# A new order table for an attention and gated-MLP kernel: 419 of 1883 operations at other places on their engines

## The chip, the cores and the metric

The kernel runs on one core of a Trainium2 chip. The metric is the device time of one execution in microseconds, taken as the median of several runs; lower is better. The engines are called TensorE (PE; its weight load is PEld), VectorE (DVE), ScalarE (ACT), GpSimd (POOL) and SyncE (SP, which issues the DMAs).

## The reference

Causal attention over 4 batches, 12 heads, 448 positions and 64 dimensions a head, and behind it a gated MLP (d_model 768, d_ff 1024) on the attention's output, all in float32:

```python
scores = scale * np.matmul(q, k.transpose(0, 1, 3, 2))
scores = np.where(mask, -1000000000.0, scores)
attn = np.exp(scores - np.max(scores, axis=-1, keepdims=True))
attn = attn / (np.sum(attn, axis=-1, keepdims=True) + 1e-09)
x = (attn @ v)   # heads side by side: (4, 448, 768)
h = x @ w_in                                   # 768 -> 1024
h = 0.5 * h * (1.0 + np.tanh(c * (h + 0.044715 * h ** 3)))
u, v = (h[..., :d_ff // 2], h[..., d_ff // 2:])
v_n = (v - mu) / np.sqrt(var + 1e-06) * g_ln   # over the 512 columns
v_s = np.einsum('ts,bsd->btd', w_sg, v_n) + b_sg[None, :, None]
return x + (u * v_s) @ w_out
```

## The kernel before

**Attention.** The 48 heads are worked on as 24 pairs, six to a batch (`pair(p)`). For a pair, TensorE makes the scores (L431), VectorE adds the mask and takes the maximum (L446), ScalarE takes the exponential with its sum (L454). VectorE turns the sums into reciprocals (L464 to L466), which go through DRAM (L473, L476) to come back as rows `rb`. The probabilities are transposed by TensorE for the first eight pairs (L498, evicted at L503 and L505) and by VectorE's stream transpose with four DMAs for the others (L486, L490). TensorE multiplies with v (L524), VectorE scales with `rb` into `xt` (L551). `keep_x` then splits `xt` into a high part (L557 on GpSimd in batch 0, L559 on ScalarE behind it) and low parts on GpSimd (L560, L562).

**Gated MLP.** `mlp(b)` runs after the six pairs of a batch in the code, and beside the pairs of the next batch in the table. All its products are made of high and low parts, three matmuls for one, through `group` (L579), in pieces of three matmuls. There are four v chunks of rows (three of 128, the last of 64), four u chunks, four groups of the spatial mix (weights `vn` of all four v chunks, against `wsg`) and six output groups. The gelu is four steps: square on ScalarE (L587), VectorE (L588), tanh on ScalarE (L590), VectorE (L592). The last v chunk is joined from two halves first (L613 on ScalarE, L615 on VectorE). The layer norm of a v chunk is a chain over three engines: statistics (L619, L620) and L621 on VectorE, a power on GpSimd (L623), L625 on VectorE, the normalising on ScalarE (L628), the high part on ScalarE (L632; L637 for the last chunk), and the low part on GpSimd (L633) for the first three chunks, but on VectorE (L638) for the last. The spatial mix needs all of these; its results go through L671 (VectorE), L675 (GpSimd), L677 (ScalarE) and L678 (GpSimd). The residual is summed on GpSimd (L691), added to the output group on VectorE (L704), and stored by DMA (L708).

**Weights.** They are loaded and split in the first 105 us: L364, L366, L368, L370, L373, L374 for the input and output weights, L352 and L353 for the spatial weights.

**What sets the order.** Each `od.add` above records an operation with its engine and what it reads and writes. Nothing is emitted until the end, where `run` goes through the numbers of the table ORDER (L67 and the lines below it) and emits operation after operation. So each engine's queue is the table restricted to its operations, each engine works strictly in that order, and buffers and PSUM banks are handed out in that order too.

Of the kernel before, what the change touches and what calls it, by code (L numbers as in the profile page):

```python
# [66 lines left out]
    0, 1, 3, 4, 84, 85, 125, 2, 89, 87, 90, 96, 86, 126, 127, 12, 18, 166, 24, 344, 350, 116, 157, 207, 88, 95, 98,  # L67
    97, 91, 93, 92, 99, 94, 101, 130, 128, 14, 129, 103, 132, 100, 13, 15, 16, 17, 134, 104, 102, 105, 106, 133, 131,
    30, 248, 356, 107, 136, 19, 110, 108, 109, 138, 140, 111, 135, 141, 167, 171, 169, 20, 168, 5, 6, 26, 21, 22, 23,
    173, 172, 170, 137, 142, 143, 145, 139, 144, 146, 7, 8, 9, 10, 114, 115, 112, 11, 149, 25, 27, 28, 29, 208, 178,  # L70
    177, 113, 180, 179, 174, 181, 31, 175, 176, 182, 184, 185, 186, 150, 210, 211, 218, 183, 32, 33, 34, 35, 117, 118,
    119, 120, 121, 122, 123, 124, 209, 216, 151, 152, 153, 190, 212, 214, 215, 217, 187, 220, 154, 222, 147, 36, 37,
    223, 213, 219, 155, 156, 224, 226, 225, 221, 227, 191, 358, 362, 364, 346, 38, 42, 44, 39, 40, 41, 584, 249, 253,
    251, 158, 159, 160, 161, 289, 148, 162, 163, 164, 585, 165, 192, 196, 194, 233, 193, 195, 234, 231, 235, 232, 236,
    228, 254, 260, 197, 252, 259, 237, 238, 250, 257, 290, 198, 255, 258, 256, 292, 291, 296, 293, 294, 262, 188, 48,
    49, 623, 50, 51, 261, 298, 52, 264, 265, 263, 268, 267, 266, 300, 43, 302, 53, 297, 304, 299, 305, 306, 239, 199,
    200, 240, 229, 54, 189, 241, 242, 243, 201, 202, 203, 204, 206, 205, 664, 308, 269, 295, 301, 440, 274, 278, 279,
    272, 441, 230, 244, 45, 46, 47, 245, 246, 247, 309, 276, 307, 303, 310, 332, 335, 338, 368, 270, 280, 321, 313,
    273, 314, 315, 316, 319, 320, 275, 317, 318, 624, 628, 626, 629, 625, 632, 630, 665, 333, 334, 336, 277, 635, 339,
    637, 337, 340, 442, 311, 631, 638, 640, 669, 627, 670, 634, 642, 351, 636, 633, 281, 282, 283, 284, 271, 285, 322,  # L80
    323, 324, 325, 374, 375, 376, 56, 370, 667, 668, 312, 326, 286, 287, 327, 328, 666, 673, 671, 672, 674, 352, 55,
    57, 639, 345, 363, 365, 347, 60, 66, 353, 62, 643, 641, 644, 354, 355, 458, 443, 676, 678, 675, 61, 647, 330, 380,
    386, 705, 744, 648, 677, 680, 459, 444, 341, 445, 446, 447, 679, 684, 63, 377, 388, 681, 682, 683, 655, 696, 645,
    685, 686, 448, 449, 58, 68, 382, 67, 357, 359, 69, 348, 349, 651, 649, 653, 460, 654, 461, 462, 463, 464, 690,
    691, 650, 646, 783, 392, 687, 398, 59, 70, 72, 706, 707, 342, 360, 361, 343, 366, 367, 404, 465, 708, 652, 466,
    712, 713, 709, 467, 710, 714, 711, 720, 722, 716, 718, 724, 717, 450, 468, 451, 469, 470, 452, 688, 689, 369, 476,
    477, 478, 479, 480, 692, 693, 694, 719, 695, 715, 723, 387, 721, 725, 481, 482, 371, 729, 745, 746, 749, 747, 753,
    748, 755, 453, 471, 751, 64, 65, 78, 754, 762, 757, 760, 764, 454, 455, 752, 483, 381, 759, 71, 288, 389, 656,
    697, 657, 658, 659, 660, 735, 410, 698, 699, 700, 329, 701, 750, 730, 731, 733, 734, 472, 378, 379, 372, 373, 416,
    422, 732, 456, 457, 484, 485, 756, 758, 383, 74, 406, 73, 79, 761, 75, 394, 76, 77, 384, 385, 784, 785, 792, 790,  # L90
    786, 494, 495, 496, 497, 498, 499, 726, 727, 486, 787, 405, 473, 80, 487, 793, 788, 763, 393, 399, 474, 475, 500,
    791, 798, 794, 395, 400, 488, 81, 489, 789, 501, 502, 82, 83, 390, 391, 490, 768, 396, 397, 491, 796, 423, 801,
    492, 493, 503, 769, 504, 505, 512, 522, 513, 514, 523, 424, 418, 425, 506, 507, 407, 428, 430, 412, 401, 532, 542,
    524, 533, 534, 535, 536, 525, 543, 526, 515, 516, 517, 544, 545, 546, 661, 795, 429, 797, 411, 508, 431, 413, 417,
    419, 402, 420, 403, 663, 802, 527, 518, 528, 800, 509, 510, 822, 1044, 434, 519, 520, 529, 511, 521, 765, 432,
    552, 537, 560, 561, 562, 538, 530, 539, 540, 531, 799, 553, 554, 555, 331, 547, 548, 556, 563, 770, 772, 736, 737,
    738, 739, 773, 771, 807, 774, 775, 776, 777, 778, 426, 408, 409, 433, 414, 557, 415, 662, 541, 549, 564, 803, 808,
    435, 421, 565, 427, 550, 551, 558, 559, 566, 823, 824, 831, 827, 825, 832, 838, 826, 436, 437, 829, 766, 728, 568,
    569, 570, 740, 830, 833, 835, 840, 842, 813, 852, 571, 576, 572, 577, 837, 839, 841, 438, 439, 567, 573, 828, 834,
    836, 578, 579, 580, 581, 1045, 1047, 1046, 586, 587, 574, 575, 582, 702, 583, 1053, 1051, 804, 811, 812, 810, 809,  # L100
    846, 847, 1048, 1055, 1057, 703, 1052, 1061, 1049, 1050, 1059, 1056, 1063, 591, 599, 600, 601, 592, 602, 767, 704,
    779, 597, 603, 588, 589, 593, 594, 1054, 595, 1062, 843, 1058, 604, 605, 606, 607, 1083, 1122, 1084, 805, 1161,
    598, 590, 608, 1085, 1123, 1088, 1086, 1087, 1060, 741, 743, 611, 780, 1064, 782, 1094, 848, 849, 850, 806, 851,
    1092, 1089, 1095, 1097, 1093, 1099, 1101, 1096, 844, 845, 814, 815, 816, 817, 853, 854, 1074, 1068, 1069, 1070,
    1073, 855, 856, 1113, 1072, 1125, 1126, 1133, 1135, 1071, 612, 617, 618, 619, 620, 613, 614, 615, 742, 818, 1090,
    1091, 1098, 781, 1127, 1128, 857, 610, 819, 1103, 621, 1124, 1129, 1162, 1100, 1102, 1104, 1131, 1105, 1163, 1200,
    609, 1134, 1136, 1065, 1066, 1132, 616, 1239, 1107, 1108, 1111, 861, 862, 863, 864, 820, 865, 858, 859, 1138, 866,
    867, 1170, 1166, 1171, 1179, 868, 1130, 869, 1177, 1181, 1140, 1137, 879, 870, 871, 872, 1168, 1167, 873, 1173,
    874, 1169, 1164, 880, 881, 882, 883, 884, 885, 1178, 886, 887, 1142, 1141, 1175, 1139, 897, 898, 899, 900, 901,
    902, 915, 916, 903, 1165, 1172, 1176, 1180, 1174, 888, 904, 905, 1110, 1109, 1112, 1146, 1067, 1106, 596, 1075,  # L110
    1114, 1115, 1076, 1077, 1078, 1147, 1150, 1148, 1149, 1151, 1116, 1117, 860, 821, 1079, 1118, 889, 875, 890, 876,
    906, 907, 891, 908, 909, 877, 878, 1201, 1202, 1240, 1207, 1143, 1208, 1205, 917, 918, 919, 920, 1206, 892, 893,
    1242, 894, 895, 896, 1209, 1210, 1185, 1203, 1144, 1152, 1191, 1186, 1190, 1189, 1217, 1212, 1214, 1204, 921,
    1216, 1215, 1219, 922, 923, 1182, 1244, 933, 934, 935, 936, 937, 943, 938, 944, 945, 946, 953, 947, 948, 963, 964,
    1005, 1080, 910, 911, 912, 913, 914, 1082, 924, 1245, 925, 1243, 1251, 1220, 1253, 1250, 1211, 926, 1213, 954,
    955, 956, 957, 965, 939, 940, 949, 927, 950, 928, 929, 1006, 1081, 1188, 1187, 1218, 951, 1224, 1225, 1221, 966,
    958, 1153, 1154, 1155, 1192, 1018, 1461, 1500, 1145, 1183, 1184, 1193, 1194, 1156, 1195, 1230, 1269, 1226, 1229,
    1228, 1227, 941, 1252, 1119, 1120, 1121, 1019, 967, 968, 930, 931, 942, 932, 959, 969, 952, 973, 974, 975, 976,
    977, 1157, 1158, 960, 961, 970, 971, 962, 978, 972, 979, 981, 982, 983, 984, 985, 989, 990, 1196, 1241, 1462,
    1463, 1248, 1249, 1255, 1257, 1246, 1247, 1222, 1539, 1259, 1256, 1254, 1258, 986, 980, 987, 991, 992, 993, 994,  # L120
    997, 998, 999, 1000, 1001, 988, 1007, 1012, 1020, 1021, 1025, 1008, 1013, 1002, 995, 996, 1003, 1022, 1014, 1004,
    1015, 1023, 1263, 1264, 1268, 1266, 1265, 1578, 1267, 1468, 1469, 1476, 1478, 1470, 1464, 1465, 1472, 1474, 622,
    1260, 1471, 1477, 1480, 1466, 1467, 1473, 1475, 1479, 1481, 1026, 1027, 1016, 1261, 1009, 1028, 1024, 1029, 1030,
# [644 lines left out]
```

## Time and profile before

| | us |
|---|---|
| median of 3 runs | 337.73 (336.57 to 338.04) |
| profiled execution, its own time | 336.46 |
| span of the profiled execution | 334.7 |
| TensorE busy in it | 323.1 |
| VectorE, ScalarE, GpSimd busy | 253.4, 207.9, 173.5 |

The profile is of one execution; its own time is 1.8 us above its span. Times in rows count from the start of the span. A row of a timeline gives start, duration, engine, line, operation and shape, and in brackets how long the engine was idle before and what ended that. TensorE is the engine with the most work and is idle for 11.6 us of the span.

### The profile page before, as it was taken

Reading aid. Unit: us, or ns where it says so; the run is one execution under the profiler, and the core shown is the slowest. Engines: PE = TensorE matmul, PEld = TensorE weight load, DVE = VectorE, ACT = ScalarE, POOL = GpSimd, SP = SyncE. Lnnn points to the kernel's source line nnn. Section 1 sums busy time; section 2 is a strip of 40 time slices with the busy share of each in tenths; the row PEclk is TensorE's granted clock in tenths of the full one; section 3 lists DMA queues with packets and bytes.
Section 4 is the critical chain, followed back from the end, with each engine's and each line's share of the span. In section 5 each row is a group of like instructions: output and inputs, shape, how many; then the busy total and the mean of one; then the engine's idle time right before and its main releaser. Section 6 shows DMA issues by size and latency. Waiting matters only on the chain.

```text
span 334.7 us, 7589 instructions
## 1 busy us (share of the span) xinstructions
PE 323.1 (97%) x2591; PEld 265.6 (79%) x2591; DVE 253.4 (76%) x762; ACT 207.9 (62%) x674; POOL 173.5 (52%) x225
## 2 busy tenths in 40 slices
PE   5799999999999999999989999999999999999995
PEld 3467768768988978878878987878988888889994
DVE  4998989999999897879698778778899422547503
ACT  3999999898857566565865537583686301465400
POOL 4366795686879852103474627051527805062690
PEclk9999999999999999999999999999999999999998
DMA  6988989587757856947757397658345451010104
GB/s 217 358 277 264 282 210 292 165 254 173 207 156 183 254 159 162 285 130 187 178 175 191 46 299 181 176 168 209 98 128 153 101 152 58 0 55 2 55 0 166
DMA packets 34326, 56.95 MB, mean 170 GB/s; under 512 B 9456, under 2 KB 18416, under 8 KB 34288
## 3 DMA queue, kind: packets, MB, share of 16 engines
q1 hardware_dynamic: 34288, 56.47, 59.4%
q8 instruction: 20, 0.33, 0.4%
q14 instruction: 18, 0.15, 0.1%
HBM read 33.39 MB, written 6.29 MB: 119 GB/s over the span
## 4 chain that ended last, share of the span: by engine, by line
PE 83%; DVE 7%; ACT 4%; DMA 3%; issue 1%; POOL 1%; SPq 0%; DVEq 0%; ACTq 0%; POOLq 0%
PE m L579 61%; PE o L524 10%; PE s L431 10%; ACT P L454 3%; DMA rb<-rd 2%; PE tx L498 1%; DMA qk<-in_qk_dram 1%; PE ty L498 1%; DVE s L446 1%; DVE vn L638 1%; DVE g L368 1%; DVE P L486 1%; DVE vn L370 1%; DVE xt L551 1%; POOL win L374 0%
## 5 line engine op out<-in xcount | busy, mean ns | idle before, releaser
L454 ACT ACTIVATE P<-s,ngm 64x64 f32<-64x64 f32 (+3 forms) x240 | 101.1, 436 | 32.5 <-DVE ngm L446 27.8
L446 DVE CUSTOM_DVE_ANT_0 s<-s,mask 64x64 f32<-64x64 f32 (+3 forms) x192 | 76.9, 438 | 9.7 <-PE s L431 7.8
L579 PE MATMUL m<-win,x 128*128 128x512 f32 (+1 forms) x264 | 65.7, 397 | 0.0
L579 PE MATMUL m<-x,win 128*128 128x448 f32 x288 | 61.7, 367 | 0.0
L579 PE MATMUL m<-g,wout 128*128 128x448 f32 x288 | 61.2, 367 | 0.0
L579 PEld LDWEIGHTS m<-x,win 128*128 128x128 f32 x288 | 54.0, 188 | 5.5
L579 PEld LDWEIGHTS m<-g,wout 128*128 128x128 f32 x288 | 53.9, 188 | 4.9
L579 PEld LDWEIGHTS m<-win,x 128*128 128x128 f32 (+1 forms) x264 | 47.2, 183 | 10.9
L431 PE MATMUL s<-qk 64*64 64x64 f32 (+5 forms) x768 | 45.3, 370 | 5.3 <-DMA qk<-in_qk_dram 4.5
L454 ACT ACTIVATION_READ_ACCUMULATOR P<-s,ngm 128x1 f32 (+1 forms) x240 | 50.3, 210 | 0.0
L431 PEld LDWEIGHTS s<-qk 64*64 64x64 f32 x768 | 29.9, 139 | 21.4 <-issue 9.5
L524 PE MATMUL o<-B,vraw 128*64 128x64 f32 (+4 forms) x672 | 45.3, 291 | 0.0
L524 PEld LDWEIGHTS o<-B,vraw 128*64 128x64 f32 x672 | 33.4, 137 | 13.1 <-issue 5.1
L486 DVE STREAM_TRANSPOSE P<-P 128x1024 f32<-128x1024 f32 x32 | 38.5, 1226 | 2.9 <-DMA B<-P 2.9
L579 PE MATMUL m<-wsg,vn 128*128 128x448 f32 x176 | 38.7, 368 | 1.2 <-DVE vn L638 1.2
L579 PEld LDWEIGHTS m<-wsg,vn 128*128 128x128 f32 x176 | 32.6, 188 | 4.6 <-DVE vn L638 1.6
L623 POOL TENSOR_TENSOR mv<-mv,mhalf 128x1 f32<-128x1 f32 (+1 forms) x16 | 10.3, 645 | 47.0 <-DVE mv L621 32.9
L560 POOL TENSOR_TENSOR x<-xt,x 128x448 fp32r<-128x448 f32 x24 | 27.4, 1149 | 12.9 <-ACT x L559 12.5
L691 POOL TENSOR_TENSOR res<-x 128x448 f32<-128x448 f32 x24 | 27.2, 1146 | 10.8 <-DMA out_dram<-res 10.8
L704 DVE TENSOR_TENSOR res<-m,res 128x448 f32<-128x448 f32 (+1 forms) x25 | 14.6, 600 | 22.3 <-PE m L579 13.6
L590 ACT ACTIVATE tmp<-tmp 128x448 f32<-128x448 f32 (+2 forms) x32 | 19.1, 601 | 15.3 <-DVE tmp L588 15.2
L588 DVE SCALAR_TENSOR_TENSOR tmp<-tmp,m 128x448 f32<-128x448 f32 (+1 forms) x28 | 17.7, 640 | 14.0 <-ACT tmp L587 13.8
(76 smaller groups left out, 395.6 us busy)
## 6 DMA issues: line engine op xcount, KB each, us to landing
B<-P SPq DMA_DIRECT2D x64, 256.0 KB
qk<-in_qk_dram SPq DMA_DIRECT2D x24, 448.0 KB
vn<-in_w_in_dram SPq DMA_DIRECT2D x12, 512.0 KB
vraw<-in_vP_dram SPq DMA_DIRECT2D x24, 256.0 KB
rb<-rd SPq DMA_DIRECT2D x24, 224.0 KB
out_dram<-res SPq DMA_DIRECT2D x9, 448.0 KB
g<-in_w_out_dram SPq DMA_DIRECT2D x16, 192.0 KB
out_dram<-res SPq DMA_DIRECT2D x5, 224.0 KB
```

Of the source, the lines that this page charges most:

```text
L431: nc.tensor.matmul(out=s[z][bk].t[64 * h:64 * h + 64, col:col + n], lhsT=qk_.t[r, 0, q0:q0 + 64], rhs=qk_.t[r, 1, k0:k0 + n], start=True, ...
L446: nc.vector.tensor_tensor_reduce(out=o, in0=i, in1=mk, scale=-0.125, scalar=3e38, op0=ALU.add, op1=ALU.min, accum_out=ngm[ib[z]][c][0:m])
L454: act(n, lambda c=c, m=m, k0=k0, n=n, bk=bk, col=col, off=off, kc=kc, i=i, z=z: nc.scalar.activation(out=P[i][0:m, off:off + n], in_=s[z][ ...
L486: dve(PW, lambda z=z: nc.vector.transpose(A[ia][:, :, :, z, :].rearrange("p g t k -> p t g k"), P[ib[z]]), Pk[z] + [kp], Ak, 1.105)
L524: nc.tensor.matmul(out=dst(o.t[r]), lhsT=vr.t[:, c, r], rhs=src(z), start=first and n == 0, stop=last and n == len(lst) - 1)
L560: pool_tt(S, lambda: nc.gpsimd.tensor_tensor(out=y.t[:, S + 64:], in0=x.t, in1=f(y.t)[:, 0:S], op=ALU.subtract), [x, y], [(y, 1)])
L579: nc.tensor.matmul(out=ps.t[0:l().shape[1], 0:n], lhsT=l(), rhs=rr(), start=(k == 0), stop=(k == len(mms) - 1))
L588: dve(n, lambda: nc.vector.scalar_tensor_tensor(out=z(), in0=z(), scalar=1.0 / GC, in1=h(), op0=ALU.add, op1=ALU.mult), [ps], [t])
L590: act(n, lambda: nc.scalar.activation(out=z(), in_=z(), func=AF.Tanh, scale=GS * GC), [], [t], True)
L623: od.add("pool", 0.46, lambda mv=mv, m=m: nc.gpsimd.tensor_tensor(out=mv.t[0:m, 1:2], in0=mv.t[0:m, 1:2], in1=mhalf[0:m], op=ALU.pow), ["s ...
L691: pool_tt(S, lambda rr=rr, x=x, k=k: nc.gpsimd.tensor_tensor(out=rr.t[:, k, :], in0=f(x.t)[:, 0:S], in1=f(x.t)[:, S + 64:], op=ALU.add), [ ...
L704: dve(hi - lo, lambda rr=rr, ps=ps, z=z, lo=lo, hi=hi: nc.vector.tensor_tensor(out=rr.t[:, z, lo:hi], in0=ps.t[:, lo:hi], in1=rr.t[:, z, l ...
```

## The change

Only the table ORDER is replaced. The program records the same 1883 operations; 419 of them stand at another place in the queue of their engine: 65 on TensorE, 147 on VectorE, 121 on ScalarE, 36 on GpSimd and 50 on SyncE. The new table comes from a search that replayed orders, half of the replays with measured and half with modelled durations and landings. Two lines of the diff, whose numbers say nothing by themselves:

```diff
 ORDER = (
-    0, 1, 3, 4, 84, 85, 125, 2, 89, 87, 90, 96, 86, 126, 127, 12, 18, 166, 24, 344, 350, 116, 157, 207, 88, 95, 98,
+    0, 4, 2, 1, 3, 84, 85, 125, 89, 86, 87, 12, 166, 18, 24, 116, 157, 344, 207, 350, 126, 90, 96, 88, 95, 91, 93, 92,
```

The first place is VectorE at the last v chunk of batch 1 (near 164 to 176 us before), where `mv` is the layer norm's mean and variance, `tmp` a gelu's working tile, `P` the probabilities and `vn` the normalised chunk. Before:

```order
474 L620 BN_AGGR mv<-st 64x2
475 L588 SCALAR_TENSOR_TENSOR tmp<-tmp,m 128x448
476 L621 TENSOR_SCALAR mv<-mv 64x1
477 L588 SCALAR_TENSOR_TENSOR tmp<-tmp,m 128x448
478 L625 TENSOR_SCALAR mv<-mv 64x1
479 L486 STREAM_TRANSPOSE P_92<-P_90 128x8x4x32 x2
480 L464 TENSOR_REDUCE tot<-sm_118 128x8
481 L465 RECIPROCAL rs<-tot 128x8
482 L466 STREAM_TRANSPOSE rT_123<-rs 128x64
483 L592 SCALAR_TENSOR_TENSOR g<-tmp,m 128x448
484 L638 TENSOR_TENSOR vn_2454<-tmp,vn_2454 64x512
```

After:

```order
479 L620 BN_AGGR mv<-st 64x2
480 L621 TENSOR_SCALAR mv<-mv 64x1
481 L588 SCALAR_TENSOR_TENSOR tmp<-tmp,m 128x448 x2
482 L486 STREAM_TRANSPOSE P_92<-P_90 128x8x4x32 x2
483 L625 TENSOR_SCALAR mv<-mv 64x1
484 L592 SCALAR_TENSOR_TENSOR g<-tmp,m 128x448
485 L464 TENSOR_REDUCE tot<-sm_118 128x8
486 L465 RECIPROCAL rs<-tot 128x8
487 L466 STREAM_TRANSPOSE rT_123<-rs 128x64
488 L638 TENSOR_TENSOR vn_2429<-tmp,vn_2429 64x512
```

L621 moved ahead of the first L588, and L625 behind the two L486. On GpSimd at the same place, before:

```order
126 L562 TENSOR_TENSOR x<-xt,x 128x64
127 L623 TENSOR_TENSOR mv<-mv,mhalf 64x1
128 L691 TENSOR_TENSOR res<-x 128x448
129 L560 TENSOR_TENSOR x<-xt,x 128x448
130 L691 TENSOR_TENSOR res<-x 128x448
131 L560 TENSOR_TENSOR x<-xt,x 128x448
132 L562 TENSOR_TENSOR x<-xt,x 128x64
133 L691 TENSOR_TENSOR res<-x 128x448
```

After:

```order
125 L562 TENSOR_TENSOR x<-xt,x 128x64
126 L691 TENSOR_TENSOR res<-x 128x448
127 L623 TENSOR_TENSOR mv<-mv,mhalf 64x1
128 L560 TENSOR_TENSOR x<-xt,x 128x448
129 L691 TENSOR_TENSOR res<-x 128x448
130 L560 TENSOR_TENSOR x<-xt,x 128x448
131 L691 TENSOR_TENSOR res<-x 128x448
132 L562 TENSOR_TENSOR x<-xt,x 128x64
```

One L691 moved ahead of L623, and the last L691 ahead of L562. On ScalarE there, the L628 and L632 of the third v chunk moved ahead of an L559. The third place is VectorE at the last v chunk of batch 2 (near 240 to 247 us before). Before:

```order
625 L619 BN_STATS st<-tmp 64x6
626 L620 BN_AGGR mv<-st 64x2
627 L621 TENSOR_SCALAR mv<-mv 64x1
628 L588 SCALAR_TENSOR_TENSOR tmp<-tmp,m 128x448
629 L446 ISA s,ngm_99<-s,mask 128x320
630 L446 ISA ngm_99 128x1
631 L625 TENSOR_SCALAR mv<-mv 64x1
632 L638 TENSOR_TENSOR vn_3225<-tmp,vn_3225 64x512
633 L588 SCALAR_TENSOR_TENSOR tmp<-tmp,m 128x448
634 L592 SCALAR_TENSOR_TENSOR g<-tmp,m 128x448
```

After:

```order
631 L619 BN_STATS st<-tmp 64x6
632 L588 SCALAR_TENSOR_TENSOR tmp<-tmp,m 128x448
633 L620 BN_AGGR mv<-st 64x2
634 L621 TENSOR_SCALAR mv<-mv 64x1
635 L446 ISA s,ngm_99<-s,mask 128x320
636 L446 ISA ngm_99 128x1
637 L625 TENSOR_SCALAR mv<-mv 64x1
638 L588 SCALAR_TENSOR_TENSOR tmp<-tmp,m 128x448
639 L638 TENSOR_TENSOR vn_3248<-tmp,vn_3248 64x512
640 L592 SCALAR_TENSOR_TENSOR g<-tmp,m 128x448
```

One L588 moved ahead of L620, the next ahead of L638, so that L592 follows L638 directly. TensorE there begins the second group of the spatial mix before the last piece of the first, which needs L638.

The other moves are small: in the first 61 us, exponentials, evictions and weight splits change places with neighbours on all engines, and SyncE issues the inputs of pair 2 earlier, and the output weights and the inputs of pair 7 later.

## Rows read from the trace of the kernel before

**Rows 1.** The page, busy time over the span: us, share, instructions.

```profile
PE 323.1 (97%) x2591; PEld 265.6 (79%) x2591; DVE 253.4 (76%) x762; ACT 207.9 (62%) x674; POOL 173.5 (52%) x225
```

**Rows 2.** Busy by stretch: PE, PEld, DVE, ACT, POOL, PEclk, DMA share, GB/s.

```profile
15.00:30.00 15.00, 14.05 (x136) 9.71 (x135) 13.57 (x53) 15.00 (x64) 8.51 (x11) 1.00 0.90 274
...
160.00:180.00 20.00, 18.81 (x142) 16.00 (x145) 15.69 (x35) 13.90 (x39) 10.28 (x12) 1.00 0.73 198
```

**Rows 3.** Waits (us, times, longest): one of the whole span, one of 160:180.

```profile
PE s L431 <- DMA qk<-in_qk_dram: 4.5, 2, 3.9
...
PE m L579 <- DVE vn L638: 1.2, 1, 1.2
```

**Rows 4.** Timeline of PE, 170 to 177 us.

```profile
172.37 1.98 PE L579 MATMUL m<-wsg,vn 128*128 128x448 f32 x9
175.55 1.69 PE L579 MATMUL m<-wsg,vn 128*128 128x448 f32 x7 [1.19 <-DVE vn L638]
```

**Rows 5.** Timeline of DVE, 162 to 176 us.

```profile
164.04 0.17 DVE L620 BATCH_NORM_AGGREGATE mv<-st 64x2 f32<-64x6 f32 x1
...
167.83 0.62 DVE L588 SCALAR_TENSOR_TENSOR tmp<-tmp,m 128x448 f32<-128x448 f32 x1 [3.62 <-ACT tmp L587]
168.37 0.14 DVE L621 TENSOR_SCALAR mv<-mv 64x1 f32<-64x1 f32 x1
...
169.34 2.37 DVE L486 STREAM_TRANSPOSE P<-P 128x1024 f32<-128x1024 f32 x2
...
172.83 2.67 DVE L638 TENSOR_TENSOR vn<-tmp,vn 64x512 fp32r<-64x512 f32 x1
```

**Rows 6.** Timeline of POOL, 164 to 176 us.

```profile
165.84 0.32 POOL L562 TENSOR_TENSOR x<-xt,x 128x64 fp32r<-128x64 f32 x1
168.59 0.54 POOL L623 TENSOR_TENSOR mv<-mv,mhalf 64x1 f32<-64x1 f32 x1 [2.42 <-DVE mv L621]
...
172.43 1.15 POOL L560 TENSOR_TENSOR x<-xt,x 128x448 fp32r<-128x448 f32 x1
...
173.82 1.13 POOL L691 TENSOR_TENSOR res<-x 128x448 f32<-128x448 f32 x1
```

**Rows 7.** Timeline of ACT, 160 to 172 us.

```profile
162.57 0.58 ACT L559 ACTIVATE x<-xt 128x448 fp32r<-128x448 f32 x1 [0.86 <-PE m L579]
...
167.28 0.95 ACT L587 ACTIVATE tmp<-m 128x448 f32<-128x448 f32 x2
...
170.31 0.56 ACT L559 ACTIVATE x<-xt 128x448 fp32r<-128x448 f32 x1
170.78 0.80 ACT L628 ACTIVATE tmp<-tmp,mv 64x512 f32<-64x512 f32 x1
171.61 0.64 ACT L637 ACTIVATE vn<-tmp 64x512 fp32r<-64x512 f32 x1
```

**Rows 8.** The executions of L638: ns min/median/max, first and last start.

```profile
L638 DVE TENSOR_TENSOR vn<-tmp,vn x4: 684/1414/2666, 94.3 to 307.2; 64x512 fp32r<-64x512 f32 x4
```

**Rows 9.** Chain that ended last, near 60 us: start, us, what.

```profile
60.15 0.58 DVE tmp L592
...
60.78 0.99 PE s L431 x16
```

**Rows 10.** The executions of L368 on `g` tiles: ns min/median/max.

```profile
L368 DVE TENSOR_SCALAR g<-g x16: 244/254/1211, 26.7 to 104.5; 128x192 int32<-128x192 int32 x16
```

**Rows 11.** Timelines of DVE, POOL and PE in batch 2, 232 to 250 us.

```profile
232.37 0.68 DVE L615 TENSOR_TENSOR tmp<-m,tmp 64x512 f32<-64x512 f32 x1 [0.87 <-ACT tmp L613]
...
242.42 2.25 POOL L691 TENSOR_TENSOR res<-x 128x448 f32<-128x448 f32 x2
...
243.12 2.10 DVE L638 TENSOR_TENSOR vn<-tmp,vn 64x512 fp32r<-64x512 f32 x1 [1.70 <-ACT vn L637]
...
245.79 0.62 DVE L592 SCALAR_TENSOR_TENSOR g<-tmp,m 128x448 f32<-128x448 f32 x1
...
244.31 4.64 PE L579 MATMUL m<-wsg,vn 128*128 128x448 f32 x22
```

178 rows, old and new, of the table ORDER are left out of this document.

## The prediction

> **What bounds the kernel now.** I read the page's first part, then the busy time by stretch, then the waits, then the timelines of the engines around the one wait that is left. TensorE is busy for 323.1 of 334.7 us [rows 1], so 11.6 us are all that any order of the same work can win. In the stretch from 160 to 180 us it is busy for 18.81 of 20 us [rows 2], at a granted clock of 1.00, and the list of waits there gives one cause for the gap: 1.2 us in which the matmuls of the spatial mix wait for L638 on VectorE, once [rows 3]. The reader should see in TensorE's timeline that nine of those matmuls end at 172.37 + 1.98 = 174.35 us and that the next seven start at 175.55 us [rows 4].
>
> The start of the program is another regime. From 15 to 30 us TensorE is busy for 14.05 us and ScalarE for 15.00 of 15 [rows 2]: there ScalarE has no idle time to fill, and since every operation still runs, moving them buys little. What is slack-free is VectorE's L592 at 60.15 us, from which the chain goes to scores on TensorE at 60.78 us with nothing between but 0.05 us [rows 9].
>
> So this change can be worth something at the 1.2 us, little before that, and it can lose where TensorE runs without a gap.
>
> **The change part by part.** No instruction is added or removed; 419 of 1883 operations stand elsewhere on their own engine, most of them by a few places.
>
> *The last v chunk of batch 1 (VectorE, GpSimd, ScalarE, 162 to 176 us).* Before, L621 stands behind an L588 that sat 3.62 us for ScalarE's L587, so it runs at 168.37 us although its input, from L620, was there at 164.04 + 0.17 = 164.21 us [rows 5]. GpSimd's L623 then starts at 168.59 us, after 2.42 us of idleness [rows 6]. After, L621 follows L620 directly. L623 then depends only on its own queue, where one L691 is put ahead of it: L562 ends at 165.84 + 0.32 = 166.16, L691 adds 1.13, L623 0.54, so it ends at 167.83 at the latest instead of 169.13 us [rows 6]. That takes the power off the chain.
>
> The next bound is VectorE's own queue, where L625 now stands behind two L588 and two L486. The L588 wait for ScalarE. ScalarE lost 0.86 us to an L559 that waited for TensorE [rows 7]; after, L628 and L632 stand ahead of that L559 and fill the hole, and the exponentials ahead of the two L587 are about the same. I take 0.8 us: the L587 start at 166.5 instead of 167.28 [rows 7]. The first L588 starts 0.55 us behind that (167.83 less 167.28), so at 167.05, the second ends 1.2 us later at 168.25 (two at 0.62), the two L486 take 2.37 to 170.6, and L625 ends by 170.8 [rows 5]. ScalarE then needs 0.80 for L628 and 0.64 for L637 [rows 7]: 172.3 us. VectorE's work between L486 and L638 was 172.83 less 171.71, or 1.1 us [rows 5], and is done by 171.9, hidden behind ScalarE. L638 starts at about 172.3 instead of 172.83 us.
>
> How long L638 takes is the open size. Its four executions took 0.68 to 2.67 us [rows 8]. The 2.67 us one ended at 175.50, which is 0.55 us after GpSimd's unbroken run of two-input operations ended at 173.82 + 1.13 = 174.95 [rows 5, 6]; in batch 2 one took 2.10 us and ended at 245.22, again 0.55 us after a GpSimd run that ended at 242.42 + 2.25 = 244.67 [rows 11]. So the row says: L638 is held until GpSimd's run is over, and then needs 0.55 us. After, the run behind L623 is L560, L691, L560, L691, L562. The second L560 needs ScalarE's L559, which ended at 170.31 + 0.56 = 170.87 [rows 7]; I leave it there. Then 1.15, 1.13 and 0.32 [rows 6] end the run at 173.5 us. L638 ends between 173.0 (0.68 alone) and 174.0 (0.55 behind the run). TensorE asks for it at 174.35, so the wait is gone, with 0.3 to 1.3 us to spare: **less 1.2 us**. If L638 took its full 2.67 us again from 172.3, it would end at 174.97 and 0.6 us of the wait would stay; that is the upper bound of this term.
>
> The Trainium skill, "SBUF — State Buffer", section "Who interferes with whom", says that a VectorE instruction with two SBUF inputs contends with a GpSimd one that reads SBUF, that the shared ports are an exclusive lock, and that whoever issues first holds them for one instruction. By that rule L638, ready at 172.83, would have waited for the one GpSimd instruction then running only and ended by about 174.3, an estimate from that page's rule and the durations here, and there would have been no wait to remove; the trace has 175.50 and disagrees. By the rule the wait would be gone in any case after the change; by the trace up to 0.6 us can stay.
>
> *Batch 2 (236 to 250 us).* VectorE gets one L588 ahead of L620 and the next ahead of L638, and TensorE begins the second spatial group before the last piece of the first. That second group needs the bank which L592 frees at 245.79 + 0.62 = 246.41 [rows 11]. Before, TensorE was not there earlier: 22 matmuls of the mix from 244.31 in 4.64 us are 0.21 each, the first nine end at 246.2 [rows 11]. After, it is there 1.2 us sooner (what batch 1 gave), at 245.0. VectorE's chain to L592 starts from TensorE too, through the L615 that waited 0.87 us at 232.37 [rows 11], and so moves earlier by 0.87 to 1.2 us: L592 at 245.2 to 245.5, or 0.2 to 0.5 us too late. I take **plus 0.3 us**. If that chain does not move at all, TensorE waits for all 1.4 us and the gain is returned.
>
> *Start (0 to 61 us).* The small moves of exponentials, evictions and weight splits leave ScalarE's sum as it was. The sizes that can change are VectorE's L368 beside GpSimd: they take 0.254 us at the median and 1.21 at the most [rows 10], so each that gets out of GpSimd's way gives up to 0.96 us, and each that gets into it costs as much, on a stretch that hands its delay on to 60.78 us. Bounds: 0.95 us less (TensorE's idle time from 15 to 30 us [rows 2]) to 2.9 us more (three held for the most). I take **less 0.2 us**, the value near zero because the work is the same.
>
> *SP and the rest.* SP issues some loads of weights and of two pairs' inputs later. TensorE waited for the qk loads twice, 4.5 us in all, of which 3.9 are the first load [rows 3]; that first load is still the first. The later ones are issued well ahead of their use, and TensorE's queue after 60 us shows no such wait; taken at nothing. If a cover there is thin, a late load shows as a new wait on DMA, within the range. The swaps on TensorE are of neighbours and cost nothing.
>
> Sum: 1.2 less, 0.3 more, 0.2 less: 1.1 us less. The profiled execution took 336.46 us (span 334.7 and 1.8 around it), so 335.4 by it; the median of the three runs is 337.73, 1.3 above the profiled one, and I state the forecast on the median: 336.6 us.
>
> **The rivals.** *B, the start gains too.* For it: TensorE's 0.95 us of idleness in 15 to 30 us and a held L368. Against it: ScalarE is full there. It would add up to about 1 us: 2.1 us less, 335.6.
> *C, the gain is returned.* The mechanism is the L592 of batch 2 above, or an L638 held as long as before in batch 1. For it: 0.2 us (246.41 less 246.2) is already missing there before any gain. Against it: VectorE's chain starts from TensorE. Net 0.1 us less: 337.6.
> *D, slower.* In 44 to 61 us, VectorE's split instructions land beside GpSimd's run and L592 comes late at 60.15 us, where TensorE has no slack [rows 9]. It decides from the point where the delay is over 1.1 us, that is with two more L368 held for the most. With three it is 2.9 less 1.1, or 1.8 us more: 339.5. Against it: the same number of GpSimd operations is there before.
> *The change does not do what it says.* The table is the order in which instructions are emitted, so the moves are real; I leave only the 0.6 us of L638 that may stay, inside the first case's range.
>
> **How the numbers follow.** Forecast 0.46 (336.0 to 337.3), B 0.24, C 0.14, D 0.16. A measurement of this kernel can tell about 0.5% (1.7 us) from no change. Faster by more: all of B and a quarter of the forecast, 0.36. Slower by more: the upper three quarters of D, 0.12. Between: 0.52. The range leaves out the best tenth, on B's side, and the worst tenth, in D: 334.9 to 338.8 us.
>
> **What would show it.** Right: no wait of the mix on L638 near 175 us, L621 straight behind L620, L623 with less than 1 us of idleness, L638 ending at least 0.3 us before TensorE is there; TensorE's 160 to 180 us at about 20 of 20. For the give-back: a wait of TensorE on L592 near 245 us of 0.2 to 0.5 us. For D: TensorE's scores behind L592 later than 60.8 us with longer L368 ahead. The forecast is wrong if TensorE's idle sum stays at 11.6 us, or if it falls by more than 2 us.

## The result, and the profile after

The changed kernel takes 334.19 us (median of four executions, 333.91 to 334.42) where the kernel before took 337.50 (four executions, 336.57 to 338.04): a ratio of 0.9919, 95% interval 0.9895 to 0.9942. That is below my range, which began at 334.9 us, and faster by over 0.5%. Timed again beside 17 executions of the kernel before, it took 334.27 us (333.90 to 334.40) against 336.56 (335.92 to 338.17): 0.9931, interval 0.9915 to 0.9947. So the change is worth 2.3 us; the first median of the kernel before stood about 0.9 us high. The executions of the kernel before scatter over 2 to 3 us, those of the changed kernel over 0.5, and this scatter is part of the story.

The profiled execution took 334.14 us (span 332.4). Busy time over the span, which answers [rows 1], and the stretch from 160 to 180 us, which answers [rows 2]:

```profile
PE 322.5 (97%) x2590; PEld 266.1 (80%) x2591; DVE 251.6 (76%) x762; ACT 207.5 (62%) x674; POOL 173.4 (52%) x225
...
160.00:180.00 20.00, 20.00 (x183) 17.07 (x183) 16.02 (x41) 13.97 (x38) 11.78 (x12) 1.00 0.76 209
```

TensorE's idle time fell from 11.6 to 9.9 us and its busy time by 0.6 us with the same work. In 160 to 180 us it has no idle time any more. TensorE's timeline of the spatial mix in batch 1, then in batch 2 (against [rows 4, 11]):

```profile
171.31 5.02 PE L579 MATMUL m<-wsg,vn 128*128 128x448 f32 x24
...
242.01 4.72 PE L579 MATMUL m<-wsg,vn 128*128 128x448 f32 x22
```

There is no bracket, so no idle time in front of them: the wait on L638 is gone in batch 1, and no wait on L592 has come in batch 2. The three other engines around the last v chunk of batch 1, VectorE, GpSimd and ScalarE in this order (against [rows 5 to 7]):

```profile
163.40 0.15 DVE L621 TENSOR_SCALAR mv<-mv 64x1 f32<-64x1 f32 x1
165.79 1.15 DVE L588 SCALAR_TENSOR_TENSOR tmp<-tmp,m 128x448 f32<-128x448 f32 x2 [2.25 <-ACT tmp L587]
166.85 2.36 DVE L486 STREAM_TRANSPOSE P<-P 128x1024 f32<-128x1024 f32 x2
169.14 0.17 DVE L625 TENSOR_SCALAR mv<-mv 64x1 f32<-64x1 f32 x1
...
170.86 1.02 DVE L638 TENSOR_TENSOR vn<-tmp,vn 64x512 fp32r<-64x512 f32 x1 [0.42 <-ACT vn L637]
...
163.99 1.14 POOL L691 TENSOR_TENSOR res<-x 128x448 f32<-128x448 f32 x1
165.10 0.54 POOL L623 TENSOR_TENSOR mv<-mv,mhalf 64x1 f32<-64x1 f32 x1
...
170.17 1.16 POOL L691 TENSOR_TENSOR res<-x 128x448 f32<-128x448 f32 x1
171.28 0.78 POOL L562 TENSOR_TENSOR x<-xt,x 128x64 fp32r<-128x64 f32 x1
...
165.22 0.96 ACT L587 ACTIVATE tmp<-m 128x448 f32<-128x448 f32 x2
...
170.19 0.64 ACT L637 ACTIVATE vn<-tmp 64x512 fp32r<-64x512 f32 x1
```

L621 runs straight behind L620, L623 has no idle time in front of it, ScalarE's two L587 come 2.1 us earlier than before, L638 starts at 170.86 and ends at 171.88. TensorE asks for it after nine of its 24 matmuls, at 171.31 + 9 x 0.209 = 173.2 us.

### The profile page after: what moved, and what is told of

Its sections match the earlier page's. It is cut to its first block, busy times and chain, and to the rows that moved or that the text cites. A ratio compares the mean times of both kernels' runs of the same rounds, so it can differ in the third digit from the quotient of the medians.

```text
span 332.4 us, 7578 instructions
## 1 busy us (share of the span) xinstructions
PE 322.5 (97%) x2590; PEld 266.1 (80%) x2591; DVE 251.6 (76%) x762; ACT 207.5 (62%) x674; POOL 173.4 (52%) x225
## 4 chain that ended last, share of the span: by engine, by line
PE 91%; ACT 6%; DMA 1%; DVE 1%; issue 0%; DVEq 0%; ACTq 0%
PE m L579 65%; PE o L524 12%; PE s L431 10%; ACT P L454 5%; PE ty L498 2%; PE tx L498 1%; DMA qk<-in_qk_dram 1%; ACT B L505 1%; ACT vn L366 1%; DVE s L446 0%; DVE res L704 0%; DVE ngm L446 0%; DVEq L446 0%; ACTq L454 0%
## 5 line engine op out<-in xcount | busy, mean ns | idle before, releaser
L454 ACT ACTIVATE P<-s,ngm 64x64 f32<-64x64 f32 (+3 forms) x240 | 102.3, 461 | 31.0 <-DVE ngm L446 25.1
L446 DVE CUSTOM_DVE_ANT_0 s<-s,mask 128x192 f32<-128x192 f32 (+3 forms) x192 | 76.7, 438 | 11.6 <-PE s L431 10.6
L579 PE MATMUL m<-win,x 128*128 128x512 f32 (+1 forms) x264 | 65.2, 396 | 0.0
L579 PE MATMUL m<-x,win 128*128 128x448 f32 x288 | 61.2, 367 | 0.0
L579 PE MATMUL m<-g,wout 128*128 128x448 f32 x288 | 61.1, 367 | 0.0
L579 PEld LDWEIGHTS m<-x,win 128*128 128x128 f32 x288 | 54.0, 188 | 5.2
L579 PEld LDWEIGHTS m<-g,wout 128*128 128x128 f32 x288 | 53.9, 188 | 4.8
L579 PEld LDWEIGHTS m<-win,x 128*128 128x128 f32 (+1 forms) x264 | 47.3, 183 | 10.9
L454 ACT ACTIVATION_READ_ACCUMULATOR P<-s,ngm 128x1 f32 (+1 forms) x240 | 55.3, 236 | 0.0
L486 DVE STREAM_TRANSPOSE P<-P 128x1024 f32<-128x1024 f32 x32 | 38.7, 1228 | 6.0 <-ACT P L454 3.8
L579 PE MATMUL m<-wsg,vn 128*128 128x448 f32 x176 | 38.2, 368 | 0.0
L560 POOL TENSOR_TENSOR x<-xt,x 128x448 fp32r<-128x448 f32 x24 | 27.5, 1149 | 17.5 <-ACT x L559 17.2
L623 POOL TENSOR_TENSOR mv<-mv,mhalf 128x1 f32<-128x1 f32 (+1 forms) x16 | 8.9, 560 | 51.5 <-DVE mv L621 51.5
L579 PEld LDWEIGHTS m<-wsg,vn 128*128 128x128 f32 x176 | 32.8, 188 | 2.9 <-DVE g L592 0.2
L691 POOL TENSOR_TENSOR res<-x 128x448 f32<-128x448 f32 x24 | 27.3, 1149 | 9.3 <-DMA out_dram<-res 9.2
L588 DVE SCALAR_TENSOR_TENSOR tmp<-tmp,m 128x448 f32<-128x448 f32 (+1 forms) x28 | 17.7, 641 | 14.2 <-ACT tmp L587 14.1
```

What stands on the lines that cost most here:

```text
L446: nc.vector.tensor_tensor_reduce(out=o, in0=i, in1=mk, scale=-0.125, scalar=3e38, op0=ALU.add, op1=ALU.min, accum_out=ngm[ib[z]][c][0:m])
L454: act(n, lambda c=c, m=m, k0=k0, n=n, bk=bk, col=col, off=off, kc=kc, i=i, z=z: nc.scalar.activation(out=P[i][0:m, off:off + n], in_=s[z][ ...
L486: dve(PW, lambda z=z: nc.vector.transpose(A[ia][:, :, :, z, :].rearrange("p g t k -> p t g k"), P[ib[z]]), Pk[z] + [kp], Ak, 1.105)
L560: pool_tt(S, lambda: nc.gpsimd.tensor_tensor(out=y.t[:, S + 64:], in0=x.t, in1=f(y.t)[:, 0:S], op=ALU.subtract), [x, y], [(y, 1)])
L579: nc.tensor.matmul(out=ps.t[0:l().shape[1], 0:n], lhsT=l(), rhs=rr(), start=(k == 0), stop=(k == len(mms) - 1))
L588: dve(n, lambda: nc.vector.scalar_tensor_tensor(out=z(), in0=z(), scalar=1.0 / GC, in1=h(), op0=ALU.add, op1=ALU.mult), [ps], [t])
```

## The experiments

Each kernel is an order table. The old and the new table hold the same operations in their first 1016, 1164 and 1445 places (TensorE is then at about 149, 175 and 224 us), so pieces can be exchanged there; in the first 482 places (67 us) one operation differs, and it stays with the old order. Each kernel was timed beside the kernel before, whose medians were 336.45 (35 executions, beside e1 to e4), 336.56 (17, beside e5 to e8), 336.89 (18, beside e9 to e11) and 337.05 (12, beside e12). The ratio is the one on record; it is not the quotient of the two medians and differs from it by up to 0.2%. Where the two part, the text says by which one it goes.

| kernel | us, median | lowest to highest | ratio to before, interval |
|---|---|---|---|
| e5_after: the changed kernel | 334.27 | 333.90 to 334.40 | 0.9931 (0.9915 to 0.9947) |
| e1_start: new to 67 us only | 336.82 | 335.57 to 338.34 | 0.9998 (0.9978 to 1.0017) |
| e7_nostart: new from 67 us | 334.61 | 334.45 to 335.16 | 0.9945 (0.9929 to 0.9960) |
| e2_b1: new in 149 to 175 us only | 335.33 | 334.16 to 336.78 | 0.9959 (0.9939 to 0.9979) |
| e8_nob1: new except 149 to 175 us | 335.66 | 335.32 to 336.35 | 0.9973 (0.9960 to 0.9986) |
| e6_to_p19: new in 149 to 224 us only | 334.85 | 334.75 to 335.38 | 0.9951 (0.9936 to 0.9966) |
| e9_p19: new in 175 to 224 us only | 336.26 | 335.74 to 337.32 | 0.9980 (0.9960 to 1.0000) |
| e12_nop19: new except 175 to 224 us | 334.28 | 333.65 to 335.56 | 0.9924 (0.9897 to 0.9951) |
| e3_l621: one operation moved | 335.57 | 334.94 to 336.72 | 0.9968 (0.9949 to 0.9987) |
| e11_l621_p19: that and 175 to 224 us | 334.86 | 334.49 to 336.14 | 0.9935 (0.9908 to 0.9963) |
| e4_pool: two GpSimd operations moved | 337.02 | 335.80 to 338.07 | 1.0006 (0.9985 to 1.0026) |
| e10_dma: changed kernel, two DMAs moved | 335.03 | 334.56 to 335.71 | 0.9925 (0.9896 to 0.9955) |

**How much is it?**

```diff
 ORDER = new
```

> The changed kernel itself, timed again beside the kernel before with many more executions of both. Theory (the 2.3 us between the two profiled executions are its worth, and the 3.3 us between the first medians held a good deal of luck in the four executions of the kernel before): 1.8 to 2.4 us less than before, a ratio of 0.993 to 0.995. Rival (the medians were right): 3.3 us less, 0.990.

Measured: 2.3 us less, 0.9931. The theory holds: the profiles had told the size better than the first medians.

**The wait on L638: put in alone, and taken out.**

```diff
-ORDER = old
+ORDER = old[:1016] + new[1016:1164] + old[1164:]
```

> The old order everywhere, but the new one for the operations between about 149 and 175 us (all moves around the last v chunk of batch 1). Theory: the wait of the spatial mix on L638 is gone and nothing of it is given back in batch 2, whose order is the old one: 1.2 to 1.4 us less than the kernel before. Rival (the gain is given back at L592 in batch 2): 0.2 us less, with a new wait near 245 us.

```diff
-ORDER = new
+ORDER = new[:1016] + old[1016:1164] + new[1164:]
```

> The changed kernel with the old order for the operations between about 149 and 175 us. Theory: the 1.2 us wait on L638 is back and nothing else changes: 1.2 to 1.4 us slower than the changed kernel, 0.5 to 0.9 us faster than before. Rival (the gain is in the DMAs of pair 19 and not in the wait on L638): less than 0.5 us slower than the changed kernel.

Taken out of the changed kernel, the piece costs 335.66 - 334.27 = 1.4 us, and the wait is back word for word (timeline of TensorE in e8_nob1):

```profile
171.22 1.98 PE L579 MATMUL m<-wsg,vn 128*128 128x448 f32 x9
174.40 1.89 PE L579 MATMUL m<-wsg,vn 128*128 128x448 f32 x8 [1.19 <-DVE vn L638]
```

Put alone into the old order, it wins 1.4 us by the ratio (1.1 by the medians), but the executions scatter over 2.6 us. The profiled one was the slowest of them, and its timeline of TensorE, and the chain that ended last, show where the gain went in it:

```profile
223.31 1.99 PE L524 MATMUL o<-B,vraw 128*64 128x256 f32 x32 [1.25 <-DMA B<-P]
...
217.55 5.52 DMA B<-P
223.07 0.24 issue
223.31 1.99 PE o L524 x32
```

That is the second half of the product of pair 19 with v, waiting for the last of its four transposing DMAs (L490): it landed at 223.07, and the product went on 0.24 us later ("issue" is time for which the profile shows no wait). I had looked for a give-back at L592 in batch 2; there was one, but here, 20 us earlier.

**One operation is enough.** On VectorE:

```diff
 L620 BN_AGGR mv<-st 64x2
+L621 TENSOR_SCALAR mv<-mv 64x1
 L588 SCALAR_TENSOR_TENSOR tmp<-tmp,m 128x448
-L621 TENSOR_SCALAR mv<-mv 64x1
 L588 SCALAR_TENSOR_TENSOR tmp<-tmp,m 128x448
```

> The kernel before with one operation moved: L621 of batch 1's last v chunk stands directly behind L620, ahead of the L588 that waits for ScalarE. Theory (GpSimd's late start and its run of two-input operations hold L638): L623 ends at about 166.7 instead of 169.1 us, GpSimd's run ends near 173.5 instead of 174.95, L638 starts at 172.7 as before and ends 0.55 us after the run, near 174.0, so TensorE waits for nothing at 174.35: 1.2 us less. Rival (VectorE's own queue, L588 and L486, sets L638): nothing changes, L638 ends at 175.5 and the wait stays.

Measured: 1.1 us less by the ratio, 0.9 by the medians. GpSimd's first and last row of the run, then L638 on VectorE, then TensorE, in this kernel:

```profile
165.79 0.54 POOL L623 TENSOR_TENSOR mv<-mv,mhalf 64x1 f32<-64x1 f32 x1
...
171.97 1.16 POOL L691 TENSOR_TENSOR res<-x 128x448 f32<-128x448 f32 x1
...
172.17 1.51 DVE L638 TENSOR_TENSOR vn<-tmp,vn 64x512 fp32r<-64x512 f32 x1
...
172.04 5.83 PE L579 MATMUL m<-wsg,vn 128*128 128x448 f32 x28
```

L638 still stands behind both L588 and both L486, as in the kernel before, and yet the wait is gone: GpSimd's run began 2.8 us earlier and was over at 173.13; L638 ended 0.55 us behind it, at 173.68. The other moves around it are not needed to end this wait.

**The run on GpSimd itself.** On GpSimd, around the run behind L623:

```diff
 L691 TENSOR_TENSOR res<-x 128x448
 L560 TENSOR_TENSOR x<-xt,x 128x448
-L691 TENSOR_TENSOR res<-x 128x448
 L560 TENSOR_TENSOR x<-xt,x 128x448
 L562 TENSOR_TENSOR x<-xt,x 128x64
-L691 TENSOR_TENSOR res<-x 128x448
 L675 TENSOR_TENSOR tmp<-tmp,g 128x448
+L691 TENSOR_TENSOR res<-x 128x448 x2
```

> The kernel before with two of GpSimd's L691 moved behind the next L675, so that the run of two-input operations behind L623 is L691, L560, L560, L562 and ends at about 172.8 instead of 174.95 us; no other queue changes. Theory (L638 is held until GpSimd's run is over): L638 starts at 172.83 as before, takes 0.7 to 1.3 us instead of 2.67, ends by 174.1, and the wait of 1.2 us is gone. Rival (L638's 2.67 us has another cause than GpSimd's run): it stays at 2.67 us and the wait stays.

The mechanism came out, the gain did not: 1.0006. The end of GpSimd's run, L638 on VectorE, a wait of ScalarE between 174 and 184 us, and TensorE at the scores of pair 18 and at pair 19; the last line is the kernel before at the scores of pair 18:

```profile
172.08 0.31 POOL L562 TENSOR_TENSOR x<-xt,x 128x64 fp32r<-128x64 f32 x1
...
172.48 0.69 DVE L638 TENSOR_TENSOR vn<-tmp,vn 64x512 fp32r<-64x512 f32 x1
...
ACT x L559 <- POOL res L691: 3.7, 1, 3.7
...
177.78 3.60 PE L431 MATMUL s<-qk 64*64 64x320 f32 x52
...
223.57 1.99 PE L524 MATMUL o<-B,vraw 128*64 128x256 f32 x32 [0.93 <-ACT P L454]
...
179.60 2.52 PE L431 MATMUL s<-qk 64*64 64x320 f32 x52
```

With the run over at 172.39, L638 takes 0.69 us where it took 2.67 [rows 5], and TensorE has no wait on it. The two L691, now behind an L675, hold up ScalarE's L559 for 3.7 us instead. Of its lead over the kernel before TensorE lost 1.1 us in the scores of pair 18 (3.60 us for what took 2.52) and 0.9 us at pair 19, where the last transposing DMA landed at 223.33, again 0.24 us ahead of the product. That the loss at pair 18 comes from the held L559 is likely and not shown.

**Pair 19.**

```diff
-ORDER = old
+ORDER = old[:1016] + new[1016:1445] + old[1445:]
```

> The old order up to 149 us, the new one from there to about 224 us (the last v chunk of batch 1 and everything up to the products of pair 19 with v), the old one behind it. Theory (in the run with the window to 175 us alone, 1.25 us of the gain went back at pair 19, whose product with v waited for the last of its transposing DMAs; the new order brings these DMAs forward by some 2 us, so the gain stays): no wait of TensorE at pair 19, 1.3 to 1.6 us less than before, a little better than the window to 175 us alone (1.1 us by the medians). Rival (those DMAs land later by chance and the new order past 175 us matters not): the same 1.1 us, with a wait on a DMA at pair 19 in the profile.

```diff
-ORDER = old
+ORDER = old[:1164] + new[1164:1445] + old[1445:]
```

> The old order, but the new one between about 175 and 224 us (from the spatial mix of batch 1 to the product of pair 19 with v). Theory (pair 19's transposing DMAs are a second, hidden limit: the old order leaves TensorE 0.24 us there, so the chance of one landing goes straight into the time): the wait of 1.2 us on L638 stays, no wait at pair 19, the median falls by only 0.2 to 0.6 us, and the executions lie within about 1 us of each other instead of over 2. Rival (the two parts are independent gains of about 1 us each): 0.9 us less or more.

```diff
-ORDER = new
+ORDER = new[:1164] + old[1164:1445] + new[1445:]
```

> The changed kernel with the old order between about 175 and 224 us (from the spatial mix of batch 1 to the product of pair 19 with v). Theory (the DMAs of pair 19 take back what TensorE has won before them, unless they are brought forward): TensorE waits 0.5 to 2 us on a DMA at pair 19, the median is 0.5 to 1.2 us over the changed kernel, and the executions scatter over more than 1 us. Rival (the order from 175 to 224 us is worth nothing by itself, as it was in front of the old order): within 0.3 us of the changed kernel.

```diff
-ORDER = e3_l621
+ORDER = e3_l621[:1164] + new[1164:1445] + old[1445:]
```

> The kernel before with L621 alone moved directly behind L620, as in the run before, and the new order between 175 and 224 us. Theory (one move wins the 1.2 us, the other keeps it): 1.5 to 1.8 us less than before, like the window from 149 to 224 us, and executions within 1 us of each other. Rival (the other moves around the last v chunk of batch 1 carry part of the gain): 1.0 us less or smaller.

On VectorE the new order puts the two L486 of pair 18 straight behind each other (1.3 us from one start to the next, 2.3 in the old order), so the moves are not only those of the first 61 us and of the two places shown. With the new order up to pair 19 (e6) there is no wait there, the gain is 1.7 us, and the executions lie within 0.6 us, against 2.6 us for the window to 175 us. With one operation and the new order from 175 to 224 us (e11) it is 2.0 us by the medians, 0.9935, but the scatter is 1.7 us: the expected calm did not come. Alone (e9) the piece wins 0.6 us by the medians, the interval of its ratio reaching to none, and the scatter of 1.6 us is again wider than I expected; the wait on L638 stayed, as it should.

The opposite kernel (e12) contradicts half of the theory. TensorE does wait there:

```profile
221.65 1.99 PE L524 MATMUL o<-B,vraw 128*64 128x256 f32 x32 [0.89 <-DMA B<-P]
```

but its median is that of the changed kernel to 0.01 us, its ratio no worse (0.9924 against 0.9931), and its best execution is the fastest of all, 333.65. So the new order from 175 to 224 us is worth nothing that can be seen on the median of the whole. The executions with it lie closer together (nine up to 334.42, against seven up to 335.56 without it); by itself the piece does not do that, as e9 and e11, which have it, scatter over 1.6 us.

All fourteen profiles say the same of the place. The second half of the product starts 1.82 us after the first half or 0.24 us after the last DMA's landing, whichever is later. With the old order from 175 to 224 us the DMA was the later one in all six profiles, by 0.1 us (the kernel before) to 1.4 us (e2_b1). With the new order it was so in four of eight: by 0.05 us in e9 and in one of the changed kernel's two profiles, 0.2 in e7 and 1.7 in e10_dma, where a DMA ahead of it is delayed. The smaller of these waits do not show in the list of waits.

The place itself was tested by a delay, on SyncE's queue of the changed kernel:

```diff
 L490 DMA B<-P_92 128x1x512 x3
-L490 DMA B<-P_92 128x1x512
 L476 DMA rb<-rd_126 128x1x448
 L518 DMA vraw<-in_vP_dram 128x512
+L490 DMA B<-P_92 128x1x512
 L518 DMA vraw<-in_vP_dram 128x512
```

> The changed kernel with two DMAs of pair 18 (the row load L476 and the v load L518) issued ahead of the last transposing DMA of pair 18 instead of behind it. Theory (pair 18's last such DMA lets pair 19's L486 start, and pair 19's DMAs let TensorE start its product at 220.7 us with no slack): that DMA is issued 1.3 us later, L486 of pair 19 starts about 1.3 us later, TensorE waits 0.8 to 1.3 us on a DMA at pair 19, and the time grows by as much, 0.8 to 1.3 us over the changed kernel. Rival (there is slack at pair 19 in the new order): the same time as the changed kernel, within 0.3 us.

L486 of pair 19 in the changed kernel, then in e10_dma, then TensorE in e10_dma:

```profile
210.62 2.37 DVE L486 STREAM_TRANSPOSE P<-P 128x1024 f32<-128x1024 f32 x2 [2.22 <-DMA B<-P]
...
212.22 2.37 DVE L486 STREAM_TRANSPOSE P<-P 128x1024 f32<-128x1024 f32 x2 [3.90 <-DMA B<-P]
222.50 1.99 PE L524 MATMUL o<-B,vraw 128*64 128x256 f32 x32 [1.50 <-ACT tmp L628]
```

L486 comes 1.6 us later and TensorE waits 1.5 us. The wait is put down to a ScalarE operation because that ended last among the semaphores; pair 19's last DMA landed at 222.26, the usual 0.24 us ahead of the product. This profiled execution was the slowest (335.71). The median is 335.03, 0.8 us over the changed kernel and the low end of what was expected, but the two were timed on different occasions, and by the ratios (0.9925 against 0.9931) nothing is lost. What speaks for a loss is that all six executions (334.56 and up) lie above all nine of the changed kernel (334.42 at most). So the delay is shown in the profile, and its price of 0.8 us rests on the medians alone.

How far landings scatter is seen at the DMA on which L486 of pair 19 waits, the last of pair 18. It landed 3.6 us after the end of its issue in the profile of the kernel before, 4.9 in e2_b1 and 4.5 in e4_pool. Counted from the issue of pair 18's first such DMA, it landed after 7.7 to 9.0 us in the six profiles with the old order from 175 to 224 us, and after 7.8 to 8.0 us in the seven with the new order that leave these DMAs alone.

**The start.**

```diff
-ORDER = old
+ORDER = (the first 482 of old, in new's order) + old[482:]
```

> The new order up to the scores of pair 9 (about the first 67 us), the old order behind it. Theory (the gain has two independent parts, both on TensorE's idle time): TensorE reaches the scores of pair 8 some 0.7 us earlier, as in the changed kernel (59.8 instead of 60.5 us), the 1.2 us wait on L638 near 175 us stays, and the profiled time falls by 0.6 to 1.0 us. Rival (the whole gain beyond the 1.2 us lies in the start, 2.1 us of the medians' 3.3): the median falls by about 2 us. Rival (the start is worth nothing and the earlier scores are noise between executions): within 0.3 us of the kernel before.

```diff
-ORDER = new
+ORDER = old[:482] + (the rest, in new's order)
```

> The changed kernel with the old order up to the scores of pair 9 (about the first 67 us). Theory (the start is worth 0.6 us where nothing behind it takes it back): 0.5 to 0.8 us slower than the changed kernel, 1.3 to 1.7 us faster than before. Rival (the start is worth nothing, as the new start in front of the old order was): as fast as the changed kernel.

In front of the old order the new start wins nothing that can be seen (0.9998); in front of the new one it wins 334.61 - 334.27 = 0.34 us, less than the 0.5 to 0.8 expected; the two kernels' executions do not overlap. What it does to TensorE is to be read at the scores of pair 8. Here they are in the changed kernel, in e7_nostart and in e11_l621_p19:

```profile
59.23 1.76 PE L431 MATMUL s<-qk 64*64 64x448 f32 x32
...
59.15 1.93 PE L431 MATMUL s<-qk 64*64 64x448 f32 x32
...
60.29 2.12 PE L431 MATMUL s<-qk 64*64 64x448 f32 x32
```

They end at 60.99, 61.08 and 62.41 us. Over all the profiles, the six with the new start end them at 60.99 to 61.19, the eight with the old start at 61.08 to 62.41, 61.7 in the mean. So the new start is about 0.5 us earlier and hardly scatters; a lucky old start is as good. A wait in front of pair 2's scores (0.63 us at 11.69 in the kernel before, on a load) is in none of the profiles with the new start, whose table issues the inputs of pair 2 earlier. But TensorE reaches the scores of pair 3 at 18.5 to 18.9 us with either start, so the gain arises behind them. Which of the moves makes it was not tested.

## Why the prediction was wrong, and where it was right

The forecast was 336.6 us, and 334.19 was measured, 2.4 less. About half of this is the base of the sum: the 337.73 us of three executions, where 17 gave 336.56. The other half is the sum of the changes: 1.1 us less was forecast and 2.3 measured. The step that failed there is the give-back of 0.3 us at L592, which did not come; L638 and the start were each priced too low, and about 0.5 us has no term.

**The wait on L638, less 1.2 us: right, 1.4 measured.** The steps happened as told, only further. L621 lost its place behind L588, L623 ended at 165.64, and the 0.86 us hole on ScalarE [rows 7] was filled. I had L638 start at 172.3; it started at 170.86, because TensorE and all that hangs on it were 1.1 us ahead by then, and the L587 were moved further than the 0.8 us I took. The slack was 1.3 us, the upper end of my 0.3 to 1.3. The 1.4 is e8_nob1 over the changed kernel, and e2_b1 by the ratio.

**How L638 is held: half right.** That GpSimd's run holds it is shown by e3 and e4. That it is held until the run is over is not the rule: in the changed kernel it ended 0.55 us after one L691, and the L562 behind that was the one that waited, 0.78 us instead of 0.32. There the trace agrees with the Trainium skill, "SBUF — State Buffer", section "Who interferes with whom", by which whoever issues first has the shared ports for the whole instruction and the other is blocked. In the kernel before and in batch 2 the trace is as I read it: in batch 2 of the changed kernel L638 again took 1.97 us, through L562 and L691. In e3_l621 one L691 was left to wait for, which fits both readings. With L691 and then L562 behind it VectorE got in between; with L560, L562, L691, with L562, L691 or with two L691 it did not. What decides this stays open.

**Plus 0.3 us at L592 in batch 2: wrong place.** VectorE's two rows there in the changed kernel:

```profile
241.14 1.97 DVE L638 TENSOR_TENSOR vn<-tmp,vn 64x512 fp32r<-64x512 f32 x1
...
243.15 0.62 DVE L592 SCALAR_TENSOR_TENSOR g<-tmp,m 128x448 f32<-128x448 f32 x1
```

L592 ends at 243.77, and TensorE's tenth matmul of the mix is due at 242.01 + 9 x 0.215 = 243.94. The chain came forward by 2.64 us (from 246.41, [rows 11]) and TensorE by 2.3. The step that failed is the bound of 0.87 to 1.2 us for the chain's advance. I took it from the one idle gap that the trace named, while the chain starts from TensorE and moves with it: in the eight profiles with the old order there, L592 ends 1.86 to 2.11 us after the mix begins, wherever that is. I also left out a move that the change itself makes, the L588 that no longer stands between L638 and L592. L592 started 0.57 us behind L638's end in [rows 11], and 0.04 us behind it here. In the six profiles with the new order L592 ends 1.76 to 1.78 us after the mix begins, and the tenth matmul is due after 1.94; the 0.17 us to spare are less than what that move gives.

**"SP and the rest, taken at nothing": the argument was wrong.** I argued from the absence of waits on DMA behind 60 us. In the kernel before, pair 19's last transposing DMA landed at 223.00 us and the second half of the product started at 223.24, the same 0.24 us later as where a wait is listed, and 1.92 us after the first half instead of 1.82. So the list of waits had no row, and yet there was no slack: 0.1 us was already lost there. (The 0.24 us of slack in the expectation of e9_p19 is this lag misread.) Any gain ahead of that place meets it. The changed kernel itself pays 0.05 us there in one profile and nothing in the other, so the term of nothing held for it; where the old order stands from 175 to 224 us, the wait was as high as 1.25 us (e2_b1), 0.93 (e4_pool) and 0.89 (e12_nop19) in one execution each.

**Less 0.2 us at the start: too small, and no constant.** It is 0.34 us of the median in the changed kernel and about 0.5 in the mean of the profiles. I took the start's one execution for its time. The held L368 that I named did go: up to 61 us the longest takes 0.66 us in the changed kernel, where one took 1.21 before. But e7_nostart still has one of 1.20 us and ends the scores of pair 8 at 61.08 us, so it is not what decides there.

**The level: wrong.** I stated the forecast on the median of three, 337.73, although the profiled execution, on which all rows rest, was 1.3 us lower. The median stood high by about a microsecond: 336.45 to 337.05 in the four later comparisons. That is half of the miss of 2.4 us. The other half, 1.2 us, is 0.2 from L638, 0.3 from the give-back that did not occur, 0.15 from the start, and about 0.5 that no term of mine had. Those 0.5 us have no single place: 0.5 by e6 against e2, none by e12 against the changed kernel, 0.2 between e7 and e6 (the order in 67 to 149 us and behind 224). Some of these differences are between kernels timed on different occasions. Where the 0.5 us lie is not settled.

Rival D (a later start through held L368) did not come. Rival C, the returned gain, did not come in the changed kernel; e4_pool shows such a return, by another road. Rival B had the sum nearly right (2.1 less), but by luck: it laid about 1 us to the start, where 0.34 is measured.

## What to carry to other kernels

Where an engine is full, the list of waits shows only the limit that binds; before a gain is booked, look behind it for the next transfer that lands within its size of the moment it is needed, and ask how far landings scatter. A tiny operation (L621, 0.14 us) that stands in an in-order queue behind an operation that waits can hold a chain over three engines: moving that one operation won a little under half of what 419 moves won (1.1 of 2.3 us, by the ratios). Take the level of the forecast from many executions, or state it as a ratio.

## What the runs showed of the hardware that I had not expected

The same matmuls do not always go at the same rate. This is the piece of 106 matmuls (L579) behind the scores of pair 10 in the chain that ended last, in the kernel before, the changed kernel, e1_start and e7_nostart:

```profile
74.40 22.37 PE m L579 x106
...
73.66 22.03 PE m L579 x106
...
73.80 22.03 PE m L579 x106
...
73.71 22.35 PE m L579 x106
```

The granted clock is 1.00 in all of them and no wait is recorded, and yet it is 22.03 us in all six profiles with the new start and 22.35 to 22.39 in the seven with the old one that show the piece: 3 ns apiece, 0.33 us. It is tempting to lay this to the start, but the eighth profile with the old start speaks against it. These are 66 of the 106 matmuls in the kernel before and in e4_pool, whose table is the old one up to 150 us:

```profile
77.20 13.79 PE L579 MATMUL m<-x,win 128*128 128x448 f32 x66
...
76.83 13.54 PE L579 MATMUL m<-x,win 128*128 128x448 f32 x66
```

So one and the same order can run at either rate. From one matmul's start to the next it is mostly 203 ns at one rate and 207 at the other, and every profile has stretches of both. What decides between them stays open, and so does whether it is part of what the start is worth.
